# Splitting every step of a recurrence-and-MLP kernel into parts issued from one table, with chosen PSUM banks and all loads on one queue

## The chip, the cores and the metric

The kernel runs on one core of one Trainium2 chip. The metric is the device time of one execution in microseconds (us). Three timed runs of the kernel before took 718.07, 716.12 and 717.27 us; the median is 717.27 us. One more execution was taken by the hardware profiler; all lines of the profile are from that one.

## The reference

Two blocks follow each other. The first is a recurrence over S = 768 time steps, for B = 4 batches and H = 8 heads with D = 40 numbers each, that is 32 independent heads, each with a state of 40x40:

```python
for t in range(S):
    y[:, :, t] = np.einsum('bhd,bhde->bhe', rt, state)
    Sa = np.einsum('bhde,bhe->bhd', state, at)
    state_decay = state * wt[:, :, None, :] - np.einsum('bhd,bhe->bhde', Sa, bt)
    state = state_decay + np.einsum('bhd,bhe->bhde', vt, kt)
```

Its output, heads side by side, is x with 3072 rows of 320. The second block is a two-layer network on these rows:

```python
h = x @ w_in                                      # 320 x 2048
g = 0.5 * h * (1.0 + erf(h * inv_sqrt2))
return (g @ w_out).astype(np.float32)             # 2048 x 320
```

r, k, v, w, a and b arrive as float32. The two weights arrive as 64-bit floats, that is as pairs of 32-bit words, and the kernel rebuilds float32 numbers from them on the chip. All products are in float32.

## The kernel before

**Tiling.** The 768 steps are cut in 12 chunks of 64. A chunk is worked for all 32 heads at once, 128 partitions being two groups of 64 rows. Inside a chunk the recurrence is turned into products of matrices: the decays are summed up by a product with a triangular mask and an exponential (`sums`, L427-452), a and b, k, r are scaled and transposed by head (`turn_*`, L520-563), and four masked 64x64 matrices per head come out of products: N (`make_N`, L598-616), A, RV and M (`masked`, L575, is the product with the mask on DVE). The state at the start of a chunk enters by `make_X` (L819) and `make_y2`; the unknown of the chunk is found with the inverse of a unit triangular matrix made from N (`make_sa` L831, `make_saT` L842); `make_QY` gives the outputs and the new state together. `outputs` (L886-897) writes xt, the transposed input of the network, with one product per half on DVE and some small DMAs that move rows between partitions, and L906-909 write the new state. `mlp` (L985-1018) is the network for the 256 rows of that chunk: four quarters of the first layer (`ph`, L993, 20 products of 64x256 each, then gelu on ACT, L995, into `gt`), then the second layer. For chunks 0 to 2 that is 32 products of 128x320 (`po`, L1010) in four quarters; from chunk 3 on it is `seven` (L937-981), seven products of halves instead of eight, with sums on DVE (L950, L960, L966) that use sums of the weights made once (`weight_sums`, L931). The prediction calls the first layer of chunk c `first(c)` and the second `second(c)`, as the changed kernel does.

**The inverse.** For chunks 1 to 11 each 64x64 matrix is cut in 32x32 blocks. N's diagonal blocks go to DRAM (L615, four stores), come back as `Nb` with one block per partition (L664, two loads), GpSimd inverts them column by column (`start_inverse`, L651-679, 62 operations at L672 and L674 into `W`), the result is stored (`store_inverse`, L686, two DMAs, on POOL's queue from chunk 3 on) and fetched into `Tt` and `T2` in its place (`fetch_inverse`, L696 and L700, six loads). `turn_corner` (L772) transposes it into `L`; `corner` (L775-787, product J, copied to `Js` at L786) and `joined` (L789-803, product J2) make the off-diagonal block. Chunk 0 does not take that path: its inverse comes from repeated squaring on PE (`squares`, L709-742, `corner_direct`, `joined_direct`).

**The weights.** `first_load` (L354-386) and `second_load` (L392-401, two issues of DMA a call) bring words of w_in and w_out to spare places; `to_float` (L312-334) rebuilds each piece with DVE (L319, L321, L324, L327, L328) and ACT (L320, L330, L331), some pieces with GpSimd (L332, L333). The words of w_out that do not fit wait in places that other tiles use: `w_out_sb` itself, `gt`, `k_rows`, a spare raw tile, a tile of `rT`. Five of the calls of `second_load` go on ACT's DMA queue, ten issues in all; all other loads are on SP's.

**What sets the order.** The kernel is under a manual schedule: every engine executes its instructions, the issues of DMA on its queue among them, in the order in which the Python code issues them. Up to chunk 2 that order is a hand-written list of calls (L1048-1242) with the network and the conversions put between as generators (`pieces`, drawn by `fill`, and `convert`); from chunk 2 on it is a loop over the chunks (L1244-1336) that issues whole steps of chunk c, of c+1 and of c+2 in a fixed sequence with one piece of the network (a quarter of a layer) at each `fill()`. What is left comes by `fill(1000)` at L1337.

**PSUM.** Every group of products gets its output from `duo` (L96-101), a pool of four buffers of [128, 2, 512] float32 handed out in turn. `keep(n)` has the next `duo` issue one extra product of n*128 columns into the buffer, a fill product that only keeps PE busy; its result is overwritten.

```python
def duo(name):
    pt = psum.tile([P, 2, 512], FP32, tag="duo", name=name)
    while asked:
        n = asked.pop()
        mm(pt[:, 0, :n * P], ident, cum_m.unsqueeze(1).to_broadcast([P, n, P]))
    return pt
```

Of the kernel before, what the change touches and what calls it, by code (L numbers as in the profile page):

```python
# [19 lines left out]
def kernel(  # L20
# [12 lines left out]

# [23 lines left out]
    asked = []  # L90

    def keep(columns):

        asked[:] = [columns]

    def duo(name):  # L96
        pt = psum.tile([P, 2, 512], FP32, tag="duo", name=name)
        while asked:
            n = asked.pop()
            mm(pt[:, 0, :n * P], ident, cum_m.unsqueeze(1).to_broadcast([P, n, P]))  # L100
        return pt

# [8 lines left out]


    def ring(name, n, shape, zero, eng):
        tiles = []
        for i in range(n):
            t = const.tile(shape, FP32, name=f"{name}{i}")
            if zero is not None:
                eng.memset(zero(t), 0.0)
            tiles.append(t)
        turn = [0]  # L120

        def take():
            turn[0] += 1
            return tiles[(turn[0] - 1) % n]
        return take
# [4 lines left out]
    def whole(t):  # L130
        return t


    def unused(t, eng):
        for x in range(2):
            eng.memset(t[x * HP + BL:(x + 1) * HP, :, BW - BL:D + BL], 0.0)


    NT = 3

    NB = 4
    NS = 3
    paired = {n: const.tile([P, G * H, BW], FP32, name=n + "_pairs") for n in ("a", "v", "r")}
    w_tile = const.tile([P, G * DM + REST], FP32, name="w_tile")


    extra = const.tile([P, 4 * G * H * HP], FP32, name="extra")
    b_rows, k_rows = ([const.tile([P, G * DM + REST], FP32, name=f"{n}_rows{i}") for i in range(2)] for n in "bk")
# [3 lines left out]

    raws = {}

    def rows_of(src, c, e):

        return src[G * e:G * (e + 1), :, c * C:(c + 1) * C, :].rearrange("g h t d -> t (g h) d")

    def fetch(c, n, src, eng, t=None):
        if t is None:  # L160
            t = rows({"b": b_rows, "k": k_rows}[n][0 if c < NB else c % 2])
        for e in range(2):
            eng.dma_start(out=t[half(e)].rearrange("p g h d -> p (g h) d")[:, :, :D], in_=rows_of(src, c, e))
        raws[c, n] = t

    def fetch_pairs(c, n, src, eng, placed, t=None):


        if t is None:
            t = paired[n]  # L170
        rows = slice(c * C // 2, (c + 1) * C // 2)
        for x in range(2):
            for z, cols in enumerate((slice(0, D + BL), slice(BL, BW))):
                to = t[x * HP + z * BL:x * HP + (z + 1) * BL, :, :cols.stop - cols.start]
                if placed:
                    for e in range(2):
                        pairs = src[G * e + x].rearrange("h (s y) d -> s h (y d)", y=2)
                        eng.dma_start(out=to[:, e::2], in_=pairs[rows, :, cols])
                else:
                    pairs = src.rearrange("b (i x) (s y) d -> x s (b i) (y d)", x=2, y=2)[x]  # L180
                    eng.dma_start(out=to, in_=pairs[rows, :, cols])
        raws[c, n] = t

    def turn(to, c, n):

        nc.vector.transpose(to.rearrange("p n (s y) -> p n y s", y=2),  # L186
                            raws.pop((c, n)).rearrange("p n (y d) -> p n y d", y=2)[:, :, :, :BL])

    def load_w(c, t=None, eng=nc.sync):
        t = w_tile if t is None else t  # L190
        to = t[:, :G * DM].rearrange("p (g h d) -> p g h d", g=G, h=H)
        if c < NB:
            fetch(c, "w", w, eng, to)
        else:
            for e in range(2):
                for g in range(G):
                    eng.dma_start(out=to[half(e ^ g), g],
                                  in_=w[G * e + g, :, c * C:(c + 1) * C].rearrange("h t d -> t h d"))
        raws[c, "w"] = t

    def by_64(t):
        return t.rearrange("p n d -> p (n d)")[:, :G * H * HP].rearrange("p (n d) -> p n d", d=HP)

    def load_a(c, t=None, eng=nc.sync):
        if c < NT:
            fetch(c, "a", a, eng, by_64(paired["a"] if t is None else t).rearrange("p (g h) d -> p g h d", g=G))
        else:
            fetch_pairs(c, "a", a, eng, False, t)

    def load_kb(c):  # L210
        fetch(c, "b", b, nc.sync)
        fetch(c, "k", k, nc.sync)

    def load_VR(c):
        VR = turned_in.setdefault(c, {})["VR"] = VR_ring()
        for e in range(2):
            nc.sync.dma_start(out=VR[half(e)].rearrange("p g q m d -> p (g q m) d")[:, :, :D], in_=rows_of(v, c, e))

    def load_v(c):
        if c >= NT:  # L220
            fetch_pairs(c, "v", v, nc.sync, True)

    def load_r(c, eng=nc.sync):
        if c >= NT:
            fetch_pairs(c, "r", r, eng, True)
            return
        t = by_64(paired["v" if c == 1 else "r"]).rearrange("p (h g) d -> p h g d", g=G)
        for e in range(2):
            for g in range(G):
                eng.dma_start(out=t[half(e), :, g, :D],  # L230
                              in_=r[G * e + g, :, c * C:(c + 1) * C].rearrange("h t d -> t h d"))
        raws[c, "r"] = t

    ctx.enter_context(tc.manual_schedule(engines={mybir.EngineType.PE, mybir.EngineType.SP,
                                                 mybir.EngineType.DVE, mybir.EngineType.Pool,
                                                 mybir.EngineType.Activation}))

    st_ring = ring("st", 1, [P, 2, NP, G, HP], lambda t: t.rearrange("p e i g d -> p (e i g) d")[:, :, D:], nc.gpsimd)
    SM_ring = ring("SM", 1, [P, 2, G, NP, VC], None, None)
    early_b = work.tile([P, NK, TB], FP32, tag="xt", name="early_b").rearrange("p k t -> p (k t)")  # L240
    early_w = SM_ring().rearrange("p e g n c -> p (e g n c)")[:, :G * DM + REST]
    early_k = work.tile([P, G, NP, P], FP32, tag="rT", name="early_k", bufs=2).rearrange("p g n t -> p (g n t)")
    ahead = {n: t[:, :G * DM].rearrange("p (g h d) -> p g h d", g=G, h=H) for n, t in (("b", early_b), ("k", early_k))}
    spare_raw = work.tile([P, 4 * DM], UINT32, tag="spare", name="spare_raw")
    early_a = spare_raw.bitcast(FP32).rearrange("p (n d) -> p n d", d=BW)

    for t in w_tile, early_w:
        nc.gpsimd.memset(t[:, G * DM:], 0.0)
    load_w(0)
    fetch(0, "b", b, nc.sync)  # L250
    load_a(0)
    load_w(1, early_w)
    fetch(1, "b", b, nc.sync, ahead["b"])
    load_a(1, early_a)
    for t in (paired["a"], early_a):
        nc.gpsimd.memset(by_64(t)[:, :, D:], 0.0)

    one = const.tile([P, 1], FP32, name="one")
    nc.vector.memset(one, 1.0)
    nc.scalar.activation(one, one, ACT.Ln)  # L260
# [1107 lines left out]
```

## Time and profile before

| what | value |
|---|---|
| timed runs | 718.07, 716.12, 717.27 us; median 717.27 |
| span of the profiled execution | 709.1 us, 32732 instructions |
| mean granted clock of TensorE | 0.958 |
| PE, matmuls | 669.7 us busy, 94% |
| PEld, weight loads | 587.1 us, 83% |
| DVE | 365.5 us, 52% |
| ACT | 222.3 us, 31% |
| POOL | 350.2 us, 49% |
| HBM | 58.69 MB read, 9.70 MB written |

The span runs from the first to the last instruction; a timed run also holds what lies around it, and the median is 8.2 us above the span. PE is TensorE with its matmuls, PEld its weight loads, which run beside them; DVE is VectorE, ACT ScalarE, POOL GpSimd, SP SyncE, and "SPq" the issues of DMA on SP's queue. L664 is line 664 of the kernel before. The page has 40 slices of 17.7 us with one digit each: tenths of busy time, or of the granted clock in the row PEclk. A group of instructions is told as line, engine, operation, output<-inputs with their shape and count, then busy time and mean duration of one in ns, then the idle time ahead of them on their engine and what ended most of it.

### The profile page before, as it was taken

How to read it: one execution, taken by the hardware profiler on the slowest of the kernel's cores; microseconds unless marked ns; L12 is line 12 of the kernel's file. 1: busy time of each engine (PE TensorE's matmuls, PEld its weight loads, DVE VectorE, ACT ScalarE, POOL GpSimd, SP SyncE). 2: the span in 40 equal slices, each digit the busy share in tenths (PEclk: the TensorE clock that was granted, in tenths of full speed). 3: DMA queues.
4: the chain of work that ended last, by engine and by line, in shares of the span. 5: the costliest groups of instructions: out<-in, count | busy, mean ns of one | idle time of the engine just before them, and what ended most of it. 6: DMA issues, size and time to landing. Idle time of an engine off the chain costs nothing.

```text
span 709.1 us, 32732 instructions
## 1 busy us (share of the span) xinstructions
PE 669.7 (94%) x14778; PEld 587.1 (83%) x14778; DVE 365.5 (52%) x481; ACT 222.3 (31%) x308; POOL 350.2 (49%) x798
## 2 busy tenths in 40 slices
PE   7578897879999999999999999999999999999997
PEld 4567786757877877899899898998998898998987
DVE  2334689993354365375484483573671772522303
ACT  5124674444140240351241332232323413112020
POOL 5284458810851851861862853845836827800000
PEclk9775798999999999999999999999999999999999
DMA  9689538864667647656656747657648646020100
GB/s 130 121 167 151 104 87 203 136 128 88 123 122 113 132 94 110 133 100 113 124 102 121 137 87 128 125 93 128 133 84 144 130 86 85 20 55 4 31 8 19
DMA packets 287923, 74.46 MB, mean 105 GB/s; under 512 B 265736, under 2 KB 284456, under 8 KB 287784
## 3 DMA queue, kind: packets, MB, share of 16 engines
q1 hardware_dynamic: 283360, 68.20, 52.6%
q0 software_dynamic: 864, 2.36, 2.2%
q8 instruction: 116, 1.90, 1.2%
q10 hardware_dynamic: 3560, 1.80, 1.0%
q14 instruction: 23, 0.19, 0.1%
HBM read 58.69 MB, written 9.70 MB: 96 GB/s over the span
## 4 chain that ended last, share of the span: by engine, by line
PE 81%; DVE 6%; DMA 3%; ACT 3%; SPq 3%; issue 2%; ACTq 1%; DVEq 0%
PE ph L993 26%; PE po L946 19%; PE po L1010 7%; PE QY L110 6%; PE J L110 2%; PE av L110 2%; PE A_ps L110 2%; PE X L110 2%; PE sq L110 2%; PE RV_ps L110 2%; DMA a_pairs<-in_a_dram 2%; PE sap L110 2%; PE saT_ps L110 2%; PE M_ps L110 2%; PE wT_ps L110 1%
## 5 line engine op out<-in xcount | busy, mean ns | idle before, releaser
L993 PE MATMUL ph<-xt,w_in_sb 64*128 64x256 f32 x1920 | 219.4, 381 | 0.0
L672 POOL TENSOR_TENSOR tmp<-W,Nb 128x126 f32<-128x126 f32 (+22 forms) x310 | 124.3, 401 | 160.0 <-DMA Nb<-N 137.0
L993 PEld LDWEIGHTS ph<-xt,w_in_sb 64*128 64x128 f32 x1920 | 182.4, 187 | 22.1 <-issue 0.3
L674 POOL TENSOR_TENSOR W<-W,tmp 128x126 f32<-128x126 f32 (+22 forms) x310 | 132.4, 427 | 24.3
L995 ACT ACTIVATE gt<-ph 128x1024 f32<-128x1024 f32 x48 | 49.1, 1024 | 152.5 <-PE ph L993 152.3
L946 PE MATMUL po<-w_out_sb,gt 128*128 128x160 f32 x576 | 83.0, 302 | 0.1
L946 PEld LDWEIGHTS po<-w_out_sb,gt 128*128 128x128 f32 x576 | 78.7, 190 | 2.2 <-DVE gt L966 0.4
L1010 PE MATMUL po<-w_out_sb,gt 128*128 128x320 f32 x192 | 55.8, 448 | 1.1 <-ACT wpT L443 1.1
L1010 PEld LDWEIGHTS po<-w_out_sb,gt 128*128 128x128 f32 x192 | 36.7, 195 | 16.7 <-issue 1.5
L186 DVE STREAM_TRANSPOSE aT<-a_pairs 128x1024 f32<-128x1024 f32 x9 | 11.2, 1247 | 46.6 <-DMA a_pairs<-in_a_dram 46.6
L802 DVE COPY Tt<-J 32x512 f32<-32x512 f32 x9 | 6.2, 689 | 54.5 <-ACT Tt L802 54.5
L786 ACT COPY Js<-J 128x256 f32<-128x256 f32 x11 | 4.1, 370 | 94.6 <-PE J L110 94.6
L998 DVE TENSOR_TENSOR half<-gt 128x1024 f32<-128x1024 f32 x9 | 11.4, 1271 | 29.6 <-ACT gt L995 29.6
L946 PE MATMUL po<-extra,half 128*128 128x160 f32 x176 | 26.1, 303 | 0.0
L320 ACT ACTIVATE conv<-conv,rebias 128x320 uint32<-128x320 uint32 (+1 forms) x26 | 16.1, 624 | 29.0 <-DVE conv L319 23.1
L575 DVE TENSOR_TENSOR SM<-M_ps,upper 128x1024 f32<-128x1024 f32 x12 | 14.5, 1207 | 19.7 <-PE M_ps L110 19.7
L946 PEld LDWEIGHTS po<-extra,half 128*128 128x128 f32 x176 | 24.2, 190 | 0.3
L995 ACT ACT_TABLE_LOAD x10 | 12.8, 1283 | 36.0 <-PE ph L993 36.0
L950 DVE TENSOR_TENSOR os<-os,po 128x160 f32<-128x160 f32 x36 | 11.5, 319 | 23.6 <-PE po L946 17.9
L946 PE MATMUL po<-extra,gt 128*128 128x160 f32 x144 | 21.0, 299 | 0.0
L662 POOL MEMSET W<- 128x512 f32 x10 | 5.3, 528 | 31.5 <-DMA inv<-W 31.5
L886 DVE TENSOR_TENSOR xt<-QY,wpT 128x512 f32<-128x512 f32 x24 | 15.4, 684 | 10.2 <-PE QY L110 9.6
(224 smaller groups left out, 1134.7 us busy)
## 6 DMA issues: line engine op xcount, KB each, us to landing
Nb<-N SPq DMA_DIRECT2D x20, 256.0 KB
VR<-in_v_dram SPq DMA_DIRECT2D x24, 160.0 KB
out_dram<-os SPq DMA_DIRECT2D x48, 80.0 KB
b_rows<-in_b_dram SPq DMA_DIRECT2D x22, 160.0 KB
k_rows<-in_k_dram SPq DMA_DIRECT2D x22, 160.0 KB
N<-N SPq DMA_DIRECT2D x44, 64.0 KB
Tt<-inv SPq DMA_DIRECT2D x44, 64.0 KB
a_pairs<-in_a_dram SPq DMA_DIRECT2D x18, 144.0 KB
```

The source lines that it names most:

```text
L110: nc.tensor.matmul(o, lhsT, rhs, start=first, stop=True, skip_group_check=True)
L320: nc.scalar.activation(power, power, ACT.Relu, bias=rebias, scale=8.0)
L575: nc.vector.tensor_tensor(to, pt, upper.unsqueeze(1).to_broadcast([P, 2 * G * NP, C]), ALU.mult)
L672: eng.tensor_tensor(t, W[:, :rows, j:j + 1].to_broadcast([P, rows, rest]), Nb[:, j:j + 1, j + 1:].to_broadcast([P, rows, rest]), ALU.mult)
L674: eng.tensor_tensor(W[:, :rows, j + 1:], W[:, :rows, j + 1:], t, ALU.add)
L886: nc.vector.tensor_tensor(xt[:, :NP, g * P:(g + 1) * P].rearrange("p i (e t) -> p i e t", e=2), Y, wp[:, g, :, :, :C], ALU.mult)
L946: nc.tensor.matmul(po[:, n, :DM // 2], l_[:, f], r_[:, f], start=f == 0, stop=f == NF // 2 - 1)
L950: nc.vector.tensor_tensor(to, one_, other, ALU.add)
L993: nc.tensor.matmul(ph[:, x, s], w_in_sb[half(x), kt, p * P:(p + 1) * P], xt[half(x), kt], start=kt == 0, stop=kt == NK - 1)
L995: nc.scalar.activation(gt[:, 4 * q:4 * q + 4].rearrange("p (x s) t -> p x s t", x=2), ph, ACT.Gelu)
L998: nc.vector.tensor_tensor(s1, block(1, 0), block(1, 1), ALU.add)
L1010: nc.tensor.matmul(po[:, g], gt[:, f, g * P:(g + 1) * P], w_out_sb[:, f], start=f == 0, stop=f == NF - 1)
```

## The change

Every step becomes a generator that yields after each small part: one DMA, one operation of an engine, or one group of products. A table written as text lists all parts of the program in the order in which they are issued, and a loop at the end runs it. An entry is `name.chunk`, with `*n` for n parts in a row, `+n` for n*128 columns of fill products, `#` and digits for the PSUM banks of the products in that part, and `@` with a letter for another engine than the part's own (s, a, v, g for SP, ACT, DVE, GpSimd).

```diff
-    asked = []
-    def keep(columns):
-        asked[:] = [columns]
+    engines = {"s": nc.sync, "a": nc.scalar, "v": nc.vector, "g": nc.gpsimd}
+    asked = {"on": None, "columns": 0, "banks": []}
+    def on(default):
+        return asked["on"] or default
+    def copy(to, given, default):
+        eng = on(default)
+        (eng.copy if eng is nc.scalar else eng.tensor_copy)(to, given)
+    def dma(to, given, default=nc.sync):
+        on(default).dma_start(out=to, in_=given)
     def duo(name):
-        pt = psum.tile([P, 2, 512], FP32, tag="duo", name=name)
-        while asked:
-            n = asked.pop()
-            mm(pt[:, 0, :n * P], ident, cum_m.unsqueeze(1).to_broadcast([P, n, P]))
+        banks = asked["banks"]
+        if banks:
+            pt = psum.tile([P, 2, 512], FP32, tag=f"duo{banks.pop(0)}", name=name, bufs=1)
+        else:
+            pt = psum.tile([P, 2, 512], FP32, tag="duo", name=name)
+        n, asked["columns"] = asked["columns"], 0
+        while n:
+            some, n = min(n, 4), n - min(n, 4)
+            mm(pt[:, 0, :some * P], ident, cum_m.unsqueeze(1).to_broadcast([P, some, P]))
         return pt
...
+    def first(c):
+        xt = xts[c]
+        for q in range(NF // 4):
+            ph = duo("ph").rearrange("p x (s t) -> p x s t", s=2)
+            for s in range(2):
...
+                        nc.tensor.matmul(ph[:, x, s], w_in_sb[half(x), kt, p * P:(p + 1) * P], xt[half(x), kt],
+                                         start=kt == 0, stop=kt == NK - 1)
+                yield
+            nc.scalar.activation(gt[:, 4 * q:4 * q + 4].rearrange("p (x s) t -> p x s t", x=2), ph, ACT.Gelu)
+            yield
...
-    for c in range(2, NCH):
-        n, n2 = c + 1, c + 2
-        more, more2 = n < NCH, n2 < NCH
-        corner(c)
-        make_X(c)
...
-    fill(1000)
+    def go(name, c, on_=None, columns=0, banks=""):
+        if (name, c) not in begun:
+            begun[name, c] = steps[name](c)
+        asked.update(on=engines.get(on_), columns=columns, banks=list(banks))
+        return next(begun[name, c], "end") != "end"
+    order = """
+        masks.0 zeros.4 load_w.0*2 zeros.2 tables.0 logs.0 masks.0 load_b.0*2 zeros.1 sums_rows.0#0+8 sums_rows.0
+        zeros.9 zeros_w.0 zeros.0 load_a.0 zeros_a.0 load_a.0 masks.0 sums.0#1+1 scale_b.0 turn_b.0#2 turn_a.0#3
+        sums.0 scale_a.0 zeros.13 turn_b.0 make_N.0#0+4 load_w.1*2 logs.1 sums.1#1+4 make_N.0 zeros.5 squares.0
...
+        turn_state.5#1 second.4#0 make_saT.6#2 turn_state.5 make_sa.6#1 make_sa.6@a load_w.8*2 second.4*2 first.5#3
...
+        second.11*7 second.11#2 second.11*3
```

The table has 1621 entries; the line with chunk 6 is one of its middle. Further:

- One of four banks (`duo0` to `duo3`, one buffer each) is named in the table for each group of products; before, the four buffers of one pool came in turn. Some work tiles that came from rotating buffers now have two fixed places in turn (`in_turn`).
- All loads are issued on SP's queue; the ten w_out issues on ACT's queue are gone from there. `store_inverse` stays on POOL's queue from chunk 3 on, and the last chunk's second half of row moves stays on ACT's.
- `mlp` is cut into `first(c)` and `second(c)`, with parts of ten products, of one gelu, of eight products, of one copy and of one output DMA each. In the table the network of chunk c stands later behind its recurrence, and in finer pieces between it.
- The parts of the first three chunks and the conversions of the weights are in another order. The squaring of chunk 0 stands ahead of most products of chunk 1; two more quarters of `first(1)` stand ahead of the second half of `second(0)`, on the half of `gt` that this does not read any more.
- Some copies run on another engine (`@v`, `@a`): some of `Tt`, `Js` and the turned state, half of saT, vT and avs of chunk 0 and some outputs go to DVE, sa of several chunks to ACT.
- Fill products stand at other places, and there are more columns of them in the head; none stands behind chunk 2.
- The arithmetic is unchanged: each kind of product, copy, mask, conversion and transfer occurs as often as before, but for the fill products.

## The prediction

> **What bounds the kernel now.** I read the page first (busy shares and slices), then the busy time by stretches, the waits of PE, and last the timelines of PE, DVE and SP for the first 175 us and for one chunk of the middle.
>
> ```profile
> span 709.1 us, 32732 instructions
> PE 669.7 (94%) x14778; PEld 587.1 (83%) x14778; DVE 365.5 (52%) x481; ACT 222.3 (31%) x308; POOL 350.2 (49%) x798
> ...
> PE   7578897879999999999999999999999999999997
> ...
> PEclk9775798999999999999999999999999999999999
> ```
>
> PE is the bound, and its slices are full from the tenth on. What is not full is the head: there PE has gaps and its clock is below 9 tenths. By stretches (columns: us, PE, PEld, DVE, ACT, POOL busy, then clock, DMA share, GB/s):
>
> ```profile
> 0.00:50.00 50.00, 34.23 (x992) 27.34 (x996) 14.57 (x17) 17.68 (x20) 26.28 (x74) 0.86 0.86 142
> 50.00:80.00 30.00, 25.29 (x721) 23.04 (x721) 14.68 (x22) 13.24 (x20) 16.28 (x34) 0.50 0.84 148
> 80.00:120.00 40.00, 34.81 (x962) 29.76 (x962) 33.91 (x44) 25.19 (x36) 24.01 (x34) 0.93 0.45 118
> 120.00:160.00 40.00, 34.03 (x594) 27.23 (x589) 37.41 (x74) 17.94 (x25) 21.52 (x50) 0.90 0.76 137
> 160.00:200.00 40.00, 38.90 (x725) 32.35 (x724) 14.22 (x24) 13.36 (x16) 20.14 (x52) 1.00 0.56 114
> 200.00:700.00 500.00, 497.71 (x10774) 442.85 (x10775) 249.21 (x299) 134.94 (x191) 241.99 (x556) 1.00 0.53 96
> ```
>
> From 200 to 700 us PE stands still for 2.3 us of 500: a new order can win nothing there and can lose. In the first 160 us busy time times clock is 34.2x0.86 + 25.3x0.50 + 34.8x0.93 + 34.0x0.90 = 105 us of full-clock work, so 55 us are lost. DVE is idle for 51 of the first 80 us and nearly full (71 of 80) from 80 to 160, when it rebuilds the float64 weights. SP issues for 131.9 of the first 160 us (its timeline, summed). The last pairs of w_out loads go out late:
>
> ```profile
> 151.69 0.98 SPq L401 DMA_DIRECT2D w_out_sb<-in_moe_w_out_dram  x2
> ...
> 155.24 1.76 SPq L401 DMA_DIRECT2D words<-in_moe_w_out_dram  x2
> ...
> 160.97 0.90 SPq L401 DMA_DIRECT2D w_out_sb<-in_moe_w_out_dram  x2
> ```
>
> and the last conversion ends at 169.4 (DVE timeline, L328). Everything after it is PE work end to end.
>
> **The work that stays.** Full-clock costs from PE's timeline past 160 us, as distance between starts: 4.5 a quarter of `first` (20 products of 64x256), 4.4 a quarter of the old `second` (8 products of 128x320), 16.3 for the seven products, 1.0 for each group of 32 small products (1.5 for a QY half, 0.7 for J or J2), 0.9 for eight transposes. Summed over the program this is 631 us without fill products, the same before and after: the counts of every kind agree. Only the fills change: 6.8 us before, 25.3 us after (the `+N` columns and `warm`), all ahead of the first `first(0)`.
>
> Before, at 169.4 PE has done chunk 0 (27.3), chunk 1 (21.5), chunk 2 to J2 (14.4), a start of chunk 3 (4.2), `first(0)` (18.1), half of `second(0)` and more (8.9), a quarter of `first(1)` (4.5): 99 us. The other 532 take 709.1 - 169.4 = 539.7, that is 7.7 of tail and small waits.
>
> **Part 1, PE order in the head.** The new table puts two more quarters of `first(1)` ahead of the second half of `second(0)`, for these need only its first half done (they overwrite `gt` 0 to 7). So 27.3 + 21.5 + 14.4 + 4.2 + 18.1 + 8.9 + 13.6 = 108 us of work can be done before the last weight is there: 9 us more than before. This gain does not depend on anything being earlier.
>
> **Part 2, when the last weight is there.** Three sums.
> SP: all loads go on its queue; ten of w_out were on ACT's. Ahead of the last w_out load stand 190 issues (176 before, with ACT's ten). By kind, from SP's rows of the head (64x16x40 loads 0.91 us, w_in 0.74 to 0.9, w_out 0.70, xt 0.73, r 1.1, N 0.62, inv 1.38): 146 us. Before, the same prices give 129.4 up to the last w_out, which really came at 161.9: 32 us of waiting, mostly where an issue stood in order for a buffer or a mask. After, the loads are cut in parts and sorted so that I find one wait that must be, N(1): its mask is due near 25 us, SP reaches it at 20, 5 us. 0.8 + 146 + 5 = 152, then 3.8 to land (the landing time that the DMA rows give for inv) and about 4.8 for two interleaved conversions (ten DVE operations of 0.32 to 0.49 and one ACT step of 0.56): 160 us.
> DVE: 103 us of work ahead of that conversion (98 before, which took 108 with POOL beside it, 10% more): 114, plus 17 idle until the first weights land near 28 us. 131, not the bound.
> PE: the squaring of chunk 0 starts before chunk 1's products instead of after them (19 instead of 24.7 us), and QY(0) is done near 72 instead of 80; between QY(0) and `first(0)` stand 15.4 us, so `first(0)` starts near 88 instead of 99.3. From there to the second half of `second(0)` 62 us of work: 150, not the bound either.
> So 160 instead of 169.4, set by SP, with PE and xt(0) (SP reaches its copies at 74) having 2 to 10 us to spare.
>
> The fills lie where PE waits: 20.5 idle us in the first 80 cover 18.5 added us, if the clock rises with them; uncovered they cost up to 18.5 (rival B). The clock row to weigh this by:
>
> ```profile
> 60.00:64.00 4.00, 3.96 (x113) 3.37 (x113) 0.84 (x2) 2.11 (x3) 2.80 (x11) 0.50 1.05 220
> ```
>
> PE is busy for 99% of these 4 us and stays at half clock, until a fill and sixteen 128-row products at 80 us; with fills among the small products (80 to 112) it stays at 1.00. I take it that the added fills hold it up, and bound it by half clock as now. [...]
>
> **Part 3, one queue.** Ten issues move from ACT to SP; 7 us more on SP, inside the 146. [...]
>
> **Part 4, the middle.** Runs of equal products change 296 times instead of 278. Two quarters of `first` together take 8.83, apart 2 x 4.52, so a change costs 0.1: 1.8 us. Fixed banks: no row shows a wait for one. Bound: nothing, to one 1.0 us evacuation per product in some chunks; I take nothing, since between a product and the next on its bank PE has several us of other work. In the table a mask waits behind what stands before it on DVE, which is half idle (249 of 500).
>
> The narrow place is the inverse. From N's product to the J that needs its inverse:
>
> ```profile
> 422.92 1.21 DVE L575 TENSOR_TENSOR N<-N_ps,upper 128x1024 f32<-128x1024 f32 x1
> 424.05 0.70 DVE L772 STREAM_TRANSPOSE L<-Tt 128x512 f32<-128x512 f32 x1
> ```
>
> N's product at 371.4, mask to 374.0, N out and back in at 383.8 (POOL waits 13.5), 31 us on POOL, stored and fetched, L done 424.75: 53.4 us. J follows at 429.3, 4.5 later. By counted PE work the distance from N to J was 58.5 and becomes 52.1 to 58 (53.8 at chunk 4, 56 for most, 52.5 and 52.1 at the last two): about 2 us of wait at the end, if the chain stays as long.
>
> **Sum.** 160 + (631 - 108) + 7.7 + 1.8 + 1 (part of the 2) = 693.5, against the span of 709.1: 15.6 us less, 9 from part 1 and 9.4 from part 2, less 2.8. The three timed runs have a median of 717.27, 8.2 above the profiled span; I keep this difference: **701.5**, by itself 696 to 706.
>
> **Rivals.**
> B, the head moves little. The clock stays at half from 50 to 80, or the fills are too long, so QY(0) is done at 80; SP stands at xt(0) until 81 instead of 74, and the last weight is ready at 167. 167 + 523 + 10.5 = 700.5, time 708.7; if it is not earlier at all, 711. For: the 60:64 row. Against: the stretch from 80 to 112.
> C, slower: the inverse's chain grows. J(c) stands 5.5 us of PE work behind N(c+1), and a chunk has 50.4 us, so nothing is lost below 55.9 and each us above it is lost on each of nine chunks. The place is SP's queue: between N's four stores, Nb's two loads and Tt's six now stand other loads, outputs and xt copies, at 0.6 to 0.9 each and in order. Six of them make the chain 58.4, nine 60: from about 57.8 the 15.6 us are gone; at 59.3, 3.4 x 9 = 31 us, 732. For: 13 us of POOL's wait are already this path. Against: other loads between N and Nb partly fill the time that SP waits for N to land (1.6 us).
> D, better: SP issues at its quickest rows (0.5 to 0.6) and PE's own 150 decides: 150 + 523 + 10.5 = 683.5, time 692. For: 0.5 a load where the DMA share is low in the middle. Against: eight loads at 1.06 each (89.6 to 98) with DMA at 0.2 to 0.5.
> E, the shares cancel (3 us a chunk late on four or five chunks): no change.
> That the table changes no order is excluded: nearly every row of every engine moves.
>
> **How the numbers follow.** A 0.44, D 0.12, B 0.16, E 0.07, C 0.21. Time 701.5. Range 687 to 726: it leaves out the better half of D and the worse part of C, together under 0.2, and holds the ends of the unknown costs (fills uncovered, the chain at 58.5). Of A, B and D all is faster by over 0.3%, about what a measurement here can tell: 0.72; E 0.07 within it; C 0.21 slower.
>
> **What would show it.** Right: `first(0)` starts near 88, the last conversion ends near 160, clock 1.00 from 50 to 80, PE idle by under 10 us past 200. Part 2 is wrong if SP shows waits in the head beyond N(1) or conversions end past 167; part 4 if PE's waits name L or Tt at J, with POOL's wait for Nb grown beyond 13 us, or any product waiting for the evacuation of its bank.

## The result and the profile after

The changed kernel takes 763.88 us (median of 4 runs, 760.56 to 769.26) where the kernel before takes 716.69 (712.95 to 718.07): 1.069 times as long, with a 95% interval of 1.063 to 1.075. The forecast was 701.5. Here and below, ratios leave out single runs over 1.5% above the fastest of their kernel: one of after_stores_on_act, one of twelve of joined_order, and two of nine of joined_order_no_fills, whose ratio with them is 1.00. The first lines of the page after, with the slices of PE and of its clock:

```profile
span 767.6 us, 32670 instructions
...
PE 697.5 (91%) x14814; PEld 597.6 (78%) x14814; DVE 382.2 (50%) x520; ACT 216.3 (28%) x277; POOL 357.5 (47%) x798
...
PE   6788889999988899888999899997999999989997
...
PEclk9899989979998999998999989999999999989999
```

PE is still the bound, but its slices are no longer full behind the tenth, and its clock falls again and again to the end of the program. The same stretches as before (us, PE, PEld, DVE, ACT, POOL busy, then clock, DMA share, GB/s):

```profile
0.00:50.00 50.00, 38.31 (x858) 25.28 (x859) 17.07 (x24) 18.02 (x22) 18.30 (x49) 0.93 0.83 128
50.00:80.00 30.00, 24.45 (x884) 19.03 (x881) 13.84 (x18) 9.39 (x13) 25.83 (x57) 1.00 0.82 148
...
160.00:200.00 40.00, 38.07 (x772) 31.27 (x774) 21.40 (x33) 8.18 (x12) 17.98 (x47) 0.93 0.63 117
200.00:700.00 500.00, 462.15 (x9999) 406.24 (x9992) 241.66 (x301) 129.58 (x162) 250.61 (x566) 0.96 0.51 95
```

From 200 to 700 us PE is idle for 37.9 us (2.3 before) and the clock is 0.96 (1.00 before). The profiled execution of the changed kernel is the slowest of its four (769.26 us), and that of the kernel before is quicker than the timed ones, so the two traces lie 58.5 us apart, the medians 47.

Where the time went is seen best as work done. I gave each PE record the full-clock cost of its kind (distance between starts in the trace of before, past 165 us, scaled to the 631 us of the prediction, fills at nothing) and summed up to a given time:

| at us | before | after | after behind by |
|---|---|---|---|
| 50 | 27.5 | 20.5 | 7.0 |
| 80 | 39.8 | 39.2 | 0.5 |
| 110 | 65.6 | 57.8 | 7.8 |
| 170 | 108.2 | 108.3 | 0 |
| 220 | 156.1 | 155.1 | 1.1 |
| 300 | 233.9 | 219.4 | 14.5 |
| 400 | 331.9 | 301.0 | 30.9 |
| 600 | 527.8 | 477.4 | 50.5 |

In these two traces the head comes out even, and some 50 us are lost from 220 to 600 us, a few in every chunk. The waits of PE past 200 us (in total, times, longest):

```profile
PE J L103 <- DVE L L814: 12.0, 3, 4.9
PE sap L103 <- DVE os L1046: 3.1, 1, 3.1
PE X L103 <- issue: 2.8, 2, 1.7
PE wT_ps L103 <- issue: 2.4, 2, 1.9
PE A_ps L103 <- ACT gt L1008: 2.3, 1, 2.3
PE M_ps L103 <- issue: 2.2, 2, 1.4
```

Gaps of over 0.15 us add up to 38.9 us: 12.0 at J, which waits for the inverse; 14.1 ended by nothing that the profile shows ("issue"); the rest, 12.8, are single waits. Besides, the clock stands at half for 41.0 us past 200 and ahead of the last product. PE is busy for 36.3 of them, so this takes another 18. Before, there were 2.1 us of such gaps past 200, and no half clock there ahead of the last product.

By the stretch of half clock that follows each wait, the loss divides in three parts of like size. Each of the three waits at J is followed by 6.8 us of half clock: about 21 us together. Three of the issue waits are followed by 3.4 us each: about 19. Behind two single waits, one for gelu and one for `os`, stand 10.2: about 17 with all the single waits. This says where PE stood, not what taking one cause away would gain.

The "issue" waits lie in the middle of a group of equal products, and nothing that the profile shows ends them. One of them in PE's timeline:

```profile
248.84 1.09 PE L103 MATMUL M_ps<-rT,saT 40*64 40x64 f32 x59
251.33 0.33 PE L103 MATMUL M_ps<-rT,saT 40*64 40x64 f32 x5 [1.39 <-issue]
251.59 0.70 PE L1005 MATMUL ph<-xt,w_in_sb 64*128 64x256 f32 x4
```

The trace's packets tell more. One DMA queue of kind "instruction" carries 116 packets of 16,384 bytes, 1.90 MB, in both kernels. PE's 14814 matmul records and as many weight loads, 29628 in all, make 255 for each packet, so by my estimate from these counts a packet is a block of some 256 of PE's instructions; in the pass of products_alone (below) beside loads, from 294.96 to 328.67 us, PE pauses eight times in a row after 128 matmuls, 256 instructions with their weight loads. Such a packet landed at 249.84 us, 1.49 ahead of the product at 251.33. Each of the 25 issue waits of over 0.3 us in the changed kernel ended 1.2 to 1.7 us after such a packet had landed; they sum to 29.3 us, 15.2 of it ahead of 200 us. Before there are eight, 5.1 us in all, 4.7 of it in the head, as two of the rows of PE's waits in the whole kernel before show:

```profile
PE sq L110 <- issue: 1.5, 2, 1.1
PE av L110 <- issue: 1.3, 3, 0.7
```

In these two traces two such packets never start less than 3.3 us apart (3.32 before, 3.48 after). In the stretch ahead of 251.33 stand sap, saT, y2 and M with only 20 records of the network among them: 542 matmul and weight-load records in 6.6 us.

**Theory**, my reading of these rows: PE's instructions come with these packets, some 256 at a time and about one packet per 3.5 us at best (3.3 to 3.5 measured), and small products in dense runs (542 records in 6.6 us) use them up. The waits cost more than their 38.9 us, since 41.0 us of half clock stand behind them. **Rivals**: the inverse's chain, lengthened by what stands between its DMAs in SP's queue (C of the prediction); the banks fixed by hand; the fills; the state that the new head leaves behind.

### The profile page after: what moved, and what is told of

Its sections match the earlier page's. It is cut to its first block, busy times and chain, and to the rows that moved or that the text cites. A ratio compares the mean times of both kernels' runs of the same rounds, so it can differ in the third digit from the quotient of the medians.

```text
span 767.6 us, 32670 instructions
## 1 busy us (share of the span) xinstructions
PE 697.5 (91%) x14814; PEld 597.6 (78%) x14814; DVE 382.2 (50%) x520; ACT 216.3 (28%) x277; POOL 357.5 (47%) x798
## 4 chain that ended last, share of the span: by engine, by line
PE 59%; SPq 10%; POOL 10%; DMA 7%; issue 7%; DVE 5%; ACT 1%; POOLq 0%; DVEq 0%; ACTq 0%
PE ph L1005 19%; PE po L1050 11%; SPq L74 10%; PE po L1029 6%; POOL W L706 5%; POOL tmp L704 4%; PE QY L103 4%; PE cum L103 2%; PE J L103 2%; PE sq L103 2%; PE wT_ps L103 1%; PE A_ps L103 1%; DMA Nb<-N 1%; PE sap L103 1%; PE M_ps L103 1%
## 5 line engine op out<-in xcount | busy, mean ns | idle before, releaser
L1005 PE MATMUL ph<-xt,w_in_sb 64*128 64x256 f32 x1920 | 237.6, 401 | 5.6 <-DMA xt<-xt 3.1
L704 POOL TENSOR_TENSOR tmp<-W,Nb 128x126 f32<-128x126 f32 (+22 forms) x310 | 128.9, 416 | 212.1 <-DMA Nb<-N 153.5
L1005 PEld LDWEIGHTS ph<-xt,w_in_sb 64*128 64x128 f32 x1920 | 193.6, 198 | 34.1 <-DMA xt<-xt 4.2
L1008 ACT ACTIVATE gt<-ph 128x1024 f32<-128x1024 f32 x48 | 49.0, 1023 | 176.3 <-PE ph L1005 176.2
L71 DVE COPY Tt<-J 32x512 f32<-32x512 f32 x12 | 8.2, 681 | 49.0 <-ACT Tt L71 40.7
L1050 PEld LDWEIGHTS po<-extra,half 128*128 128x128 f32 x176 | 25.3, 196 | 0.2
L71 ACT COPY os<-po 128x160 f32<-128x160 f32 (+1 forms) x13 | 4.0, 313 | 70.2 <-DVE os L71 37.8
L704 POOL TENSOR_TENSOR st<-st,spare_x 128x126 f32<-128x126 f32 (+22 forms) x31 | 12.4, 399 | 21.8 <-DMA spare_x<-N 19.5
L71 DVE COPY os<-po 128x160 f32<-128x160 f32 (+1 forms) x20 | 7.0, 352 | 30.6 <-PE po L1050 14.5
L610 DVE TENSOR_TENSOR N<-N_ps,upper 128x1024 f32<-128x1024 f32 x12 | 14.6, 1221 | 14.8 <-PE N_ps L103 14.8
```

Of the source, the lines that this page charges most:

```text
L71: (eng.copy if eng is nc.scalar else eng.tensor_copy)(to, given)
L610: nc.vector.tensor_tensor(to, pt, upper.unsqueeze(1).to_broadcast([P, 2 * G * NP, C]), ALU.mult)
L704: nc.gpsimd.tensor_tensor(t, W[:, :rows_, j:j + 1].to_broadcast([P, rows_, rest]), Nb[:, j:j + 1, j + 1:].to_broadcast([P, rows_, rest]), ...
L1005: nc.tensor.matmul(ph[:, x, s], w_in_sb[half(x), kt, p * P:(p + 1) * P], xt[half(x), kt], start=kt == 0, stop=kt == NK - 1)
L1008: nc.scalar.activation(gt[:, 4 * q:4 * q + 4].rearrange("p (x s) t -> p x s t", x=2), ph, ACT.Gelu)
L1050: nc.tensor.matmul(to, l_[:, f], r_[:, f], start=f == 0, stop=f == NF // 2 - 1)
```

## The experiments

The kernel before took 711.5, 710.6, 711.5 and 712.5 us (medians) in the four groups in which these runs were timed, against 716.69 beside the changed kernel. So kernels are compared here by their ratios to it, with the changed kernel at 1.069; the expectations were written in the us of its 763.88.

### Is it the order past chunk 2?

The first attempt put the changed table up to the corner of chunk 3 and then the parts that are left in the order of the kernel before:

```diff
-        ... fetch_inverse.3 corner.3 make_X.3#3 make_N.4*2 sums_rows.4 ... (the changed table)
+        corner.3 make_X.3 (a quarter) joined.3 (a quarter) make_sa.3 make_saT.3 (a quarter) make_y2.3 make_M.3 ...
```

> The changed kernel's table up to the first part of the corner of chunk 3 (about 226 us in its trace), all remaining parts in the order of the kernel before, each product group on the free bank unused for longest. Theory (the order past chunk 2 loses the time: PE waits for instructions, for the inverse, for banks, and the half clock that follows): the rest, about 471 us of work, runs at the pace of before (0.975), span 715 to 730, time 723 to 740, PE idle under 10 us past 240. Rival (the state that the changed head leaves, with the network lagging and SP late, is what costs): span stays above 750.

839.6 us, 1.179 (1.176 to 1.182), far above the theory's range. PE waited 83.2 us for the row moves of xt, 19 times: I had let the network follow its recurrence directly. The run says nothing of the theory; it shows the price of the lag that both kernels give the network.

> As the run middle_as_before, but with the network's lag of the kernel before: the first layer of chunk c now stands in chunk c+1, between its corner and its QY, and the second layer behind QY; in the first attempt it stood half a chunk earlier, and PE waited 83 us for the row moves of xt. Theory (the order past chunk 2 loses the time): 471 us of work left at about 226 us, at the pace of before, span 712 to 727, time 720 to 735, PE waits past 240 under 10 us. Rival (the state that the head leaves): span above 745.

736.8 us, 1.036 (1.034 to 1.039). Its waits of PE past 200 us:

```profile
PE po L1050 <- DVE st L965: 12.1, 7, 1.7
PE J L103 <- DVE L L814: 4.3, 1, 4.3
```

The issue waits are gone, and a new one stands in seven chunks: the network's product waits until DVE has read the state's sums from the bank that I had given to both. So this fixed bank did cost, 12.1 us of waits.

```diff
-  sums_rows.0#0+8   sums.0#1+1   make_N.0#0+4   (and so on, all fills)
+  sums_rows.0#0     sums.0#1     make_N.0#0
```

> As middle_as_before_2 without any fill product. The run after_no_fills had 7 us more of work done at 220 us than the changed kernel, and 6 more than the kernel before. Theory (head and middle add up): 6 to 8 us less than middle_as_before_2, 713 to 728, a ratio to before of 0.99 to 1.015. Rival (what the head wins is waited away at the seam): same as middle_as_before_2.

735.5 us, 1.034 (1.031 to 1.037): the rival holds here, under 2 us.

```diff
-        banks = asked["banks"]
+        banks = []
```

> As middle_as_before_2 with one pool of four PSUM buffers and no chosen bank. In middle_as_before_2 PE waited 15.6 us for the sums of the new state, about 1.9 in each chunk, at products whose bank I had fixed as the one opened longest ago. Theory (a fixed bank that is still being read costs its wait): 714 to 724, these waits gone. Rival (the order makes PE wait there, whatever the bank): 732 to 740.

722.1 us, 1.016 (1.012 to 1.020), as the theory has it: the same order with free banks is 15 us faster. Past 320 us this kernel keeps the pace of before to within 2 us. So the order from chunk 3 on accounts for most of the loss: 0.054 of the 0.069, some 38 of 49 us. Against after_free_banks below, which has the changed order with the same free banks (1.074), it is 0.058. What was left lay at the seam: SP stood 5.3 us at an output store that waited for `os`, ahead of the loads of chunk 3's inverse.

```diff
-        second.1*4 make_av.3 ... make_N.4#0 ... second.1*2 load_v.4*3 sums_rows.4 make_N.4*5 inverse.4*2 load_VR.4 ...
+        make_av.3 ... make_N.4#0 ... make_N.4*5 inverse.4*2 corner.3 zeros.6 second.1*7 load_v.4*3 sums_rows.4 load_VR.4 ...
```

> As middle_as_before_3, with the seam changed: the loads of chunk 3's inverse, N of chunk 4 with its mask, its stores and its loads, and L of chunk 3 stand ahead of the rest of second(1), whose output store had held SP's queue for 5.3 us ahead of those loads (L of chunk 3 at 225.7 us, PE waiting 4.8 us for it, then half clock; 7.4 us lost there and 4.6 us more at 300 to 320, where a load was late for the same reason). Past 320 us middle_as_before_3 ran exactly as fast as before. Theory (that one place is what is left): 8 to 12 us less than middle_as_before_3, 710 to 716, ratio 0.998 to 1.006. Rival (the head of the new order hands over a later state of SP in any case): 718 to 724.

715.4 us, 1.0036 (1.0006 to 1.0067), as the theory has it. Its middle:

```profile
200.00:700.00 500.00, 493.75 (x10746) 439.44 (x10739) 246.87 (x296) 135.31 (x190) 250.99 (x570) 1.00 0.52 97
```

The same with all fills taken out, as in the diff of middle_as_before_no_fills:

> As joined_order without fill products: if the fills of the head are paid in part (after_tiny_fills was 10 us faster than the changed kernel, 4 of it by 220 us), 3 to 6 us less than joined_order, 705 to 713, ratio 0.991 to 1.002. Rival (as between middle_as_before_2 and middle_as_before_no_fills, the head waits elsewhere): the same as joined_order.

711.3 us, 0.9957 (0.9924 to 0.9990): 0.8% less than with the fills, and the only kernel here whose interval lies below 1, by so little that I would not call it a gain. It has the new head without fills and the old middle.

### PE's instructions

A kernel of its own, which leaves out all of the reference's computation (its output is zeros) and runs a stretch of products twice, alone and then beside loads:

```diff
+    small(1024)                      # 32 groups of 64 matmul records, 40x64 by 40x64
+    large(100)                       # 200 matmul records, 64x128 by 64x256
+    for n in range(8):
+        small(64), large(20)         # two groups at a time
+    large(60)
+    for n in range(8):
+        small(128), large(20)        # four groups at a time
```

> Leaves out the whole computation: PE alone runs 32 groups of 32 small products (40x64 by 40x64) in a row, then 8 times two groups and 20 products of 64x256, then 8 times four groups and 20 such products; then all of it again beside loads of small rows. Theory (PE's instructions come in blocks of 16 KB, 256 matmuls and weight loads, not closer than 3.3 to 4.1 us): 32 groups take 55 to 70 us instead of 33, with a gap of 1.5 to 2 us every 256 instructions ended by nothing that the profile shows; two groups beside 20 products: no gaps; four groups: small gaps, under 1 us each. Rival (the stalls come from DMA traffic or from something that other engines do): 33 us and no gap in the first pass, gaps only in the second.

PE's timeline of this kernel:

```profile
39.23 4.19 PE L57 MATMUL small_ps<-rhs,lhs 40*64 40x64 f32 x271
44.94 50.45 PE L57 MATMUL small_ps<-rhs,lhs 40*64 40x64 f32 x1777 [1.51 <-issue]
95.31 23.95 PE L63 MATMUL large_ps<-rhs,lhs 64*128 64x256 f32 x200
119.19 2.10 PE L57 MATMUL small_ps<-rhs,lhs 40*64 40x64 f32 x128
121.22 4.59 PE L63 MATMUL large_ps<-rhs,lhs 64*128 64x256 f32 x40
125.73 2.09 PE L57 MATMUL small_ps<-rhs,lhs 40*64 40x64 f32 x128
...
192.89 3.60 PE L57 MATMUL small_ps<-rhs,lhs 40*64 40x64 f32 x231
197.60 0.61 PE L57 MATMUL small_ps<-rhs,lhs 40*64 40x64 f32 x25 [1.11 <-issue]
```

32 groups take 56.1 us instead of 33, with nothing on the other engines: the rival is out. Packets of instructions start 3.6 us apart on average in this run, 71 instructions per us, where two groups (128 matmuls and 128 weight loads, 256 instructions) alone take 2.1 us at full clock. The waits look otherwise than I expected: after one of 1.5 us the clock falls to half and stays there for 54.6 us. The 1777 small products behind that wait take 50.45 us, 28.4 ns each, where those of the two groups take 16.4: at half clock 128 matmuls with their loads take 3.6 us, the distance between two packets. Two groups beside 20 products have no gap; four groups have one of 0.9 to 1.6 us in seven of eight times, where I had expected under 1. Beside loads the 32 groups take 62.4 us, so traffic adds 6 us to a wait that is there without it.

Fills beside the groups where PE had waited for nothing that shows, 15 products of 512 columns at 12 places:

```diff
-        make_M.3#1   sums.5#1    make_RV.4#2    ...
+        make_M.3#1+4 sums.5#1+8  make_RV.4#2+8  ...
```

> The changed kernel with 15 fill products (15.3 us of PE work) added past chunk 2, one or two ahead of each of twelve groups of small products in or near which PE stood for nothing shown (M 3, sums 5, RV 4, M 4, A 5, sums 7, X 6, M 7, X 9, M 9, J 10, saT 11). Theory (PE has run out of instructions there, so that a fill lies beside the wait for them): such waits past 200 us fall from 16.5 to under 8, the clock drops less often, time 758 to 768. Rival (each fill is paid in full): 775 to 782.

753.4 us, 1.062 (1.057 to 1.067). 15 us of work were added, and the kernel became no slower: the ratio is 0.007 below that of the changed kernel, some 5 us, and the two intervals overlap. The issue waits past 200 us fell from 14.1 to 1.8 us, half clock (ahead of the last product) from 41.0 to 23.9.

```profile
200.00:700.00 500.00, 480.96 (x10411) 416.12 (x10410) 246.78 (x307) 130.19 (x162) 251.37 (x560) 0.98 0.50 94
```

The rival, 775 or more, is out: these fills were not paid. The 15 us added and the 5 gained make some 20, near the 19 put down to the issue waits above. The theory's reading is that a fill of four instructions lies beside the wait and keeps the clock. Another was not tested: 60 more instructions also shift where the blocks begin, and leaving instructions out did nearly as much to these waits (after_no_fills, below). Fills of hardly any time at the same places would tell the two apart.

The opposite, density put into the kernel before:

```diff
             turn_b(n2)
-        fill()
         if c == NS:
...
             store_inverse(n2, (nc.gpsimd,))
+        fill()
         if more:
             turn_corner(n)
```

> The kernel before with one piece of the network moved in the loop: from between the group of sums, A, turned state and av, and the group of RV and N, to behind N. Seven groups of small products then follow each other, the same work in all. Theory of the instruction supply: a wait of 1.5 to 3 us ended by nothing shown per chunk, 9 chunks, and a half-clock stretch behind some: 15 to 30 us slower, 732 to 748. Rival (PE takes small products at any density): within 5 us of before, or faster since N comes 4.4 us earlier.

737.4 us, 1.037 (1.032 to 1.041): the time of the theory, by another cause.

```profile
PE N_ps L110 <- DVE nT L520: 13.0, 8, 1.8
...
PE RV_ps L110 <- issue: 1.0, 2, 0.9
```

N came ahead of DVE's transpose of b. That this wait gave PE's instructions time to arrive is likely and not shown. So the run doesn't support the theory. But it gives a price: 13.0 us of waits cost 25.3 us of span, since six stretches of half clock past 200 us (23.9 us, 12 lost) stand behind them.

### Fills

The changed kernel without its fills (and without the two parts of `warm`):

```diff
-        sums_rows.0#0+8 ... sums.0#1+1 ... make_N.0#0+4 ...
+        sums_rows.0#0   ... sums.0#1   ... make_N.0#0   ...
```

> The changed kernel without any fill product (25.3 us of PE work at full clock less, all ahead of chunk 3). Theory (fills only stand in gaps and hold up the clock): the clock falls to half between 50 and 100 us as in the kernel before, time 764 to 775. Rival (they push the work behind them back): 746 to 758.

747.7 us, 1.053 (1.048 to 1.059). The rival holds: with the fills the ratio is 0.016 higher, some 12 us. But part of it came past 220 us, where no fill stands: the issue waits past 200 us were 4.2 us instead of 14.1. Hence the next run.

```diff
-            mm(pt[:, 0, :some * P], ident, cum_m.unsqueeze(1).to_broadcast([P, some, P]))
+            mm(pt[:32, 0, :1], ident[:32, :32], cum_m[:32, :1])
```

> The changed kernel with each fill product replaced by one of 32x32 by 32x1: as many instructions of PE, hardly any time (under 3 us in all). The run after_no_fills was 16 us faster than the changed kernel, 7 of it in the head, and past 220 us its waits for nothing shown were 5.3 us instead of 16.5, though no fill stands there. Theory (the blocks of 256 instructions begin elsewhere when instructions are left out ahead of them, and so do the waits): with the count as in the changed kernel these waits are back at 13 to 17 us, time 753 to 760. Rival (it was the time of the fills and what followed from it): 745 to 751, waits under 8 us.

753.9 us, 1.061 (1.057 to 1.065); issue waits past 200 us 11.1. The time is as the theory has it, the waits a little below its 13 to 17. The four traces of this order in which PE has equally many instructions have 14.1, 11.6 (after_free_banks), 8.8 (after_stores_on_act) and 11.1 us of such waits, the two with another count 4.2 and 1.8. So it looks as if where a block of 256 begins decides which group is cut; each kernel has one trace. Of the 12 us some 6 would be the time of the fills and 6 the shifted blocks, differences no larger than the intervals. With the tiny fills the clock fell to half at 42 to 56 and 66 to 80 us, and the kernel was still faster than with fills.

### Banks, the queue and the inverse

The changed kernel, with the banks in turn as before (the table names them no more, as `sums.0#1+1` becomes `sums.0+1`):

```diff
-        sums_rows.0#0+8 ... sums.0#1+1 ... turn_b.0#2 ...
+        sums_rows.0+8   ... sums.0+1   ... turn_b.0   ...
```

> The changed kernel with one pool of four PSUM buffers again, so that no product has a bank chosen for it; the order is that of the changed kernel. Theory (fixed banks cost): the waits of PE for the evacuation of another product's bank past 200 us (A_ps and QY for gelu, po for A's mask, sap for the sums of os, wT for xt: 10 us, and two half-clock stretches, 5 us) go away: 748 to 756. Rival (with four buffers that all stand open, any choice waits as long): 760 to 768.

764.4 us, 1.074 (1.071 to 1.077). The rival holds: PE's waits past 200 us are 38.0 us as against 38.9, at other products: 11.5 us are now two waits of the network's second layer for ACT's `part`, and J's fell to 4.0.

```diff
-                dma(out[row:row + C], ...)
+                dma(out[row:row + C], ..., nc.scalar)
```

> The changed kernel with the 48 stores of the output issued on ACT's queue instead of SP's. In the changed kernel SP stands behind such a store for os 7.1 us between the stores of N of chunk 5, 4.7 and 2.9 elsewhere, and stores of N start up to 15 us after their mask. Theory (SP's queue lengthens the inverse's chain and makes PE wait for L): PE's waits for L at J fall from 12.6 us to under 5, time 748 to 757. Rival (PE is late itself and the chain has room but for a few places; or ACT's gelu is then late): 760 to 770.

760.8 us, 1.067 (1.062 to 1.073): no gain. PE's waits:

```profile
PE N_ps L103 <- DVE nT L548: 7.9, 1, 7.9
PE ph L1005 <- DMA xt<-xt: 7.4, 4, 3.9
PE J L103 <- DVE L L814: 3.8, 1, 3.8
```

J's wait fell to 3.8 as the theory has it, and the two others shown grew by 13 us. In the changed kernel SP had stood like this for N of chunk 5, whose mask ended at 286.7:

```profile
286.71 0.30 SPq L74 DMA_DIRECT2D N<-N  x1
...
294.71 0.52 SPq L74 DMA_DIRECT2D out_dram<-os  x1
295.28 1.20 SPq L74 DMA_DIRECT2D N<-N  x2
...
301.21 0.62 SPq L74 DMA_DIRECT2D N<-N  x1
```

Four stores, 2.1 us of issues, take 15 us: an output store among them waits 7.1 us for `os`, and seven more DMAs stand between.

So the changed kernel was given N, its corner loads and Nb of each chunk from 3 on as one piece:

```diff
-        make_N.c#b ... make_N.c ... make_N.c*2 ... inverse.c ... inverse.c ...
+        make_N.c#b make_N.c*5 inverse.c*2 ...
```

> The changed kernel with, for chunks 3 to 11, N's mask, its four stores and the two loads of Nb directly behind N's product in the table, ahead of what stood between them on DVE (the transpose L of the chunk before, others) and on SP (output stores, pair loads, row moves). Theory (the inverse's chain is what lengthens a chunk): from N's product to L 53 to 56 us instead of 56 to 69, PE's waits for L at J under 4 us instead of 12, time 742 to 755. Rival (the chain is late because PE is late; the time is lost at PE by waits of many kinds and the half clock): 758 to 770, with the waits elsewhere.

791.5 us, 1.114 (1.109 to 1.119): slower than either expected. Both ends of the inverse's path stand in one queue: with N and Nb of the next chunk first, the loads of Tt and T2 of this one came later.

```profile
PE J L103 <- DVE L L814: 9.5, 3, 4.0
PE J L103 <- DMA T<-inv: 9.0, 5, 6.0
PE J L103 <- DMA Tt<-inv: 5.0, 4, 1.5
```

So the chain can hold PE, and pulling one end ahead delays the other. That it is the main loss of the changed kernel was not shown: with its waits cut by 8 us the time stayed.

### A try at the head of the kernel before

```diff
+    fill()
     make_QY(1)
...
-    fill()
+    fill(2)
     second_load(15, 0, spare_rT, eng=nc.sync)
```

(One `fill()` less stands behind each of the two.)

> The kernel before with two pieces of the network moved up in its head: the third quarter of first(0) ahead of QY(1), where PE stands 4.3 us for the mask of M (111 to 116 us) and then runs at half clock to 122, and the second quarter of second(0) ahead of J of chunk 2, where PE stands 2.9 us (150 to 153), then half clock to 159. Theory (an idle place filled with work that is ready saves the idle time and the half clock behind it, and the last weight at 169.4 has 6.6 us to spare): 5 to 8 us less, ratio 0.989 to 0.994. Rival (the last weight, or the wait moved to the next step, sets the end all the same): within 1.5 us of before.

713.2 us, 1.002 (0.999 to 1.005): the rival holds. Work moved into idle places of the head was waited away elsewhere in it: PE's waits from 95 to 200 us are 12.5 us, and 11.8 before.

## Why the prediction was wrong, point by point

- **What bounds the kernel, and that a new order can only lose past 200 us**: right. The failing step is the one behind it, "Part 4, the middle", put at 2.8 us in the sum. It measured about 50. The 1 us in it for J, which waits for the inverse, became 12.0 us and some 9 more at half clock. I looked for waits for data, banks and the inverse, and priced PE's small products by their rows as if they could follow each other at will. The rows of before did show otherwise: in its head, where small products stand dense, PE has seven issue waits, 4.7 us. Past 200 us a quarter of the network stands between every few groups, and one such wait is left. The issue waits were not in the sum at all; they came to 14.1 us and some 5 more at half clock.
- **No price for what a wait does to the clock.** I took a microsecond of wait as one. Past 200 us 38.9 us of waits brought some 18 us of loss at half clock; in before_groups_together 13.0 brought 12.
- **Part 2, the fills** ("20.5 idle us in the first 80 cover 18.5 added us"): wrong. The clock did stand at 1.00 from 50 to 80 us, as forecast, but the kernel is some 12 us faster without the fills, of which about half is their time; joined_order gains some 6 us without them. Ahead of their places PE often stood in an issue wait (15.2 us of them ahead of 200) or was on the way to a mask.
- **Part 2, SP**: the 190 issues took 142 us with the short gaps between them instead of 146, but SP waited 26 us on the way (gaps of over 0.1 us), not 5. The longest wait is the one I named, N(1): 11.4 us. The mask began at 33.9 instead of 25, for ahead of it PE lost 2.2 and 2.4 us to issue waits and ran fills of 4.4 us mostly at half clock. The last w_out load was issued at 168.2 and the last conversion ended at 176.3 instead of 160.
- **Part 1**: the second half of `second(0)` never waited for a weight. It began at 178.3, 2.0 us behind the last conversion, and PE's own path decided, `first(0)` starting at 103.1 instead of 88. Without the 9 us of work ahead of it that half would have begun near 169.3 and come to its last two tiles from 172.6 on, up to 3.7 us ahead of their weights; by this estimate from these times part 1 bought under 4 us, not 9.
- **Fixed banks at nothing**: right for this table (after_free_banks), and no rule: 15 us in middle_as_before_2. One sign set for part 4 did come: past 200 us products waited for a bank to be read (2.3 us for gelu, 3.1 for `os`), but with the banks in turn the waits are as long in all.
- **Rival C, the inverse's chain in SP's queue**: the sign was right, and its place is seen (15 us between N's mask and its last store). With the half clock behind its three waits it is the largest of the three parts, about 21 of some 57 us; but with its waits cut by 8 us the time stayed, so it is not the loss alone. Its chance, 0.21, was too low: I held the middle safe because I could name only one way to lose there.
- **From span to time**: I added 8.2 us, the distance of the timed median from the profiled span. In every run that has both on record the time is some 1.7 us above the span; the rest is that the timed executions were slower than the profiled one. It shifts the forecast and the kernel before alike.
- **That a table could keep the middle as full as the loop did**: shown possible by joined_order.

What stays open is how the single waits of the changed order (12.8 us at about ten places) share out between the order of DVE, ACT and SP. Only their removal together, by going back to the old order, was tried. That the issue waits, the inverse and the single waits each cost what is put down to them is read from one trace. after_fills_middle took away most of the issue waits, but added work; after_stores_on_act took away most of J's, and others grew.

## What to carry to other kernels

Count instructions as well as time: where a change packs small products closer, compare their number per microsecond with the densest run that the trace shows without a gap; the long run of small products here got 71. With the half clock behind them PE's waits cost one and a half times their length in the changed kernel (38.9 us and 18 more) and nearly twice in before_groups_together (13.0 and 12 more), so a PE-bound middle that is full is to be left alone, and a change tried on the head only. I would put a fill only where a row shows PE idle at that very place: 15 us of them beside issue waits came out some 5 us ahead, with intervals that overlap (after_fills_middle), and leaving out those of the head some 12 (after_no_fills).

## What the runs showed of the hardware

- **Instructions**: packets of 16,384 bytes, 116 of them, one for 255 of PE's matmul and weight-load records in the changed kernel; starts 3.3 us apart at the least (before), 3.6 in the steady run of products_alone; in the changed kernel PE goes on 1.2 to 1.7 us after one has landed. In products_alone small products that would use 122 instructions per us got 71, and the 32 groups took 56.1 us instead of 33.
- **The clock**: in the changed kernel all stretches of half clock past 200 us but the last, behind the last product, begin and end on a grid of 3.41 us. Eight windows of this grid had PE busy for 0.58 or less, and half clock followed all eight; the fullest, at 284.7 us, had 1.4 us of idle time. Of 20 at full clock with 0.59 to 0.88 it followed one, and of three at half clock with as much it followed all three. These windows show no sharp threshold: the one at 591.9 us, with 0.70, had half clock behind it, those at 516.8 with 0.61 and 332.5 with 0.65 full clock.
- **Half clock under a busy PE**: in products_alone it stayed for 54.6 us while PE's timeline shows small products without a gap (44.94 to 95.31 us), and it rose behind the first window that large ones filled. At half clock PE used its instructions about as fast as they were delivered, 256 in 3.6 us. Why the clock did not rise is not shown.
